# Key features interleaved by pairs of heads, a new start, shorter last sums and re-listed instructions in a four-block linear-attention and ReGLU kernel

## The chip, the cores and the metric

One core of one Trainium2 chip. The metric is device time of one execution in microseconds (us), median of several runs on chips whose runs of the kernel before agree within about 1%. All runs quoted here are of state fast. Engines: TensorE (PE in the profile), VectorE (DVE), ScalarE (ACT), GpSimd (POOL), SyncE (SP, which here issues DMA).

## The reference, cut to what matters

Four blocks on x of 2048 x 512, in bf16: attention, ReGLU, attention, ReGLU (called layers 0 to 3), each with a layer norm before and a residual after.

```
def _A_ref(x, wqkv, w_phi, wo):              # 32 heads of 16
    q, k, v = ...                            # x @ wqkv
    pq, pk = q @ w_phi, k @ w_phi            # per head
    phi_k = concat[softmax(pk), softmax(-pk)]   # over the 16 features of a head; phi_q alike
    kv = einsum("bhsf,bhsd->bhfd", phi_k, v);  z = einsum("bhsf->bhf", phi_k)
    o  = (phi_q @ kv) / (phi_q @ z + 1e-6)
    return o @ wo
def _B_ref(x, W_gate, W_up, W_down):         # F = 1376
    gate = relu(x @ W_gate);  return (gate * (x @ W_up)) @ W_down
```

All keys must be summed into kv before the first query can be answered: a barrier in each attention layer.

## The kernel before

The weights w_phi are folded into the key and query weights once (a block-diagonal BD per chunk of 128 columns). Instructions are recorded with cost figures (`ii` is the time until the engine takes the next, `lat` the time to the result) and put in order by a list scheduler when the program is built. The cost figures therefore change no instruction, but they do change the order on every engine.

The key stage, for each of 16 row tiles. Inside a chunk of 128 columns, feature f of head h sits at column 8f + h, so one head's 16 features are 8 columns (16 bytes) apart:

```python
for s in range(2):
    op("act", ... e.activation(ft.ap()[:, s, :], kt.ap(), ACT.Exp, scale=(1.0, -1.0)[s]), ...)
op("dve", ... e.tensor_reduce(zt.ap().rearrange("p (a h) -> p a h", h=8),
        ft.ap().rearrange("p s (c f h) -> p (s c) h f", f=16, h=8), AX.X, ALU.add), ..., ii=1105, lat=1185, name="Z")
op("dve", ... e.reciprocal(rt.ap(), zt.ap()), ...)
op("dve", ... e.tensor_tensor(ft..., ft..., rt.ap()...unsqueeze(2).to_broadcast([P, 8, 16, 8]), ALU.mult), ..., name="norm")
```

The barrier: sums on TensorE in four bursts of four tiles for each of three banks, then a masked copy of each of eight groups, and every R matmul (expq, the exponentials of the queries, times kvs, the masked sums) waits for all of them:

```python
for b, gs in enumerate(GROUPS):
    for q in range(4):                       # one op: 4 tiles x the bank's groups
        ...
    for j, (s, c) in enumerate(gs):          # 16 instructions in all
        op("dve", ... e.tensor_tensor(kvs[:, g, 0:128]..., pt..., mask2[:]..., ALU.mult), ...)
        op("dve", ... e.tensor_scalar(kvs[:, g, 128:136], mask2[:], pt..., 5e-7, ALU.mult, ALU.add), ...)
kvr[l] = [res(n, g) for g in range(8) for n in ("kvsn", "kvsd", "kvsm")]
```

The softmax here doesn't subtract the row's maximum and nothing guards it: scores larger than these inputs give would overflow.

## Time and profile before

442.8 us (440.2 to 444.4). The stage lengths below are read from the timeline view (start of the first, or end of the last, instruction of the kind named); the right-hand column tells which engine is full.

| stage, kernel before | from to, us | length | full engine |
|---|---|---|---|
| start, to the first key sum | 0 to 13.3 | 13.3 | none |
| layer 0's keys, to the last normalisation | 13.3 to 72.5 | 59.2 | VectorE |
| to the first gate matmul of layer 1 | 72.5 to 97.7 | 25.2 | none |
| layer 1, with the rest of layer 0, to the first key matmul of layer 2 | 97.7 to 226.9 | 129.2 | TensorE |
| layer 2's keys | 226.9 to 276.8 | 49.9 | VectorE |
| to the first gate matmul of layer 3 | 276.8 to 304.4 | 27.6 | none |
| layer 3 to the end | 304.4 to 438.1 | 133.7 | TensorE |

The windows view of the kernel before shows that. Each row is a stretch, its length, then busy us and instructions of the engines named in the first line, the share of full clock that TensorE was granted, the DMA share and GB/s:

```profile
core 0: us, PE busy (x) PEld busy (x) DVE busy (x) ACT busy (x) POOL busy (x), PEclk, DMA share, GB/s
13.26:72.47 59.21, 39.97 (x241) 21.06 (x244) 59.20 (x86) 27.68 (x58) 0.00 (x0) 0.86 0.50 130
72.47:97.69 25.22, 20.61 (x148) 11.22 (x150) 15.73 (x45) 20.03 (x64) 5.23 (x18) 1.00 0.16 32
97.69:226.92 129.23, 128.48 (x759) 70.71 (x773) 93.96 (x213) 48.21 (x165) 8.76 (x30) 1.00 0.23 43
226.92:276.79 49.87, 40.73 (x239) 22.15 (x243) 49.87 (x58) 29.77 (x62) 0.00 (x0) 0.93 0.07 14
276.79:304.35 27.56, 19.67 (x136) 10.65 (x137) 15.96 (x46) 16.22 (x56) 5.25 (x18) 0.94 0.14 29
304.35:438.10 133.75, 128.87 (x759) 70.87 (x772) 80.43 (x174) 42.50 (x138) 8.99 (x30) 1.00 0.21 46
```

VectorE is busy 59.20 of 59.21 us and 49.87 of 49.87 us in the two key stages; in the two long stages TensorE is. In the two transitions neither is full. What fills VectorE is in the groups view of the kernel before (busy us, mean ns of one, then idle time before and what ended it; `z<-phik` is the key sum, `phik<-phik,rz` the normalising multiply):

```profile
L583 DVE TENSOR_REDUCE z<-phik 128x64 f32<-128x1024 bf16 x32 | 61.2, 1948 | 2.0 <-ACT phik L582 2.0
L530 DVE BATCH_NORM_STATS2 stats<-x_sb 128x6 f32<-128x512 bf16 x64 | 42.8, 682 | 1.4 <-DMA x_sb<-in_A_x_dram 0.8
L586 DVE TENSOR_TENSOR phik<-phik,rz 128x1024 bf16<-128x1024 bf16 x32 | 20.0, 694 | 0.0
```

One key sum takes 1948 ns for 1024 elements, where bn_stats takes 682 ns for 512. The sum is the only one of the three that steps 16 bytes at each element.

The barrier, in the timeline of the kernel before (start, us, engine, line, instruction, number; in brackets the idle time before it and what ended it). The last normalisation starts at 71.76 us; the mask instructions end at 77.39 us:

```profile
71.76 0.70 DVE L586 TENSOR_TENSOR phik<-phik,rz 128x1024 bf16<-128x1024 bf16 x1
74.62 0.69 DVE L642 TENSOR_TENSOR kvs<-pb,mask 128x128 bf16<-128x128 f32 x3 [2.16 <-PE pb L631]
75.22 0.23 DVE L645 TENSOR_SCALAR kvs<-mask,pb 128x8 bf16<-128x8 bf16 x1
75.36 1.07 DVE L642 TENSOR_TENSOR kvs<-pb,mask 128x128 bf16<-128x128 f32 x5
76.35 1.04 DVE L645 TENSOR_SCALAR kvs<-mask,pb 128x8 bf16<-128x8 bf16 x7
```

### The profile page before, as it was taken

How to read it: one execution, taken by the hardware profiler on the slowest of the kernel's cores; microseconds unless marked ns; L12 is line 12 of the kernel's file. 1: busy time of each engine (PE TensorE's matmuls, PEld its weight loads, DVE VectorE, ACT ScalarE, POOL GpSimd, SP SyncE). 2: the span in 40 equal slices, each digit the busy share in tenths (PEclk: the TensorE clock that was granted, in tenths of full speed). 3: DMA queues.
4: the chain of work that ended last, by engine and by line, in shares of the span. 5: the costliest groups of instructions: out<-in, count | busy, mean ns of one | idle time of the engine just before them, and what ended most of it. 6: DMA issues, size and time to landing. Idle time of an engine off the chain costs nothing.

```text
span 438.1 us, 6374 instructions
## 1 busy us (share of the span) xinstructions
PE 384.3 (88%) x2308; PEld 210.2 (48%) x2348; DVE 322.6 (74%) x647; ACT 190.6 (44%) x556; POOL 31.6 (7%) x128
## 2 busy tenths in 40 slices
PE   3779718969999999999999966966999999999996
PEld 2323416437765545444443443624766544545442
DVE  6899998488989874636599999558897977334333
ACT  4748502966454431413149733546645443113200
POOL 3000000221110200000000000021111120000000
PEclk9969977999999999999999998889999999999999
DMA  6735930122321240112013000012342231201112
GB/s 179 170 61 87 326 107 0 25 49 49 77 57 38 60 62 12 37 24 38 13 36 62 0 1 0 1 24 49 49 86 49 48 62 37 48 13 36 25 36 72
DMA packets 69934, 24.18 MB, mean 55 GB/s; under 512 B 61360, under 2 KB 69904, under 8 KB 69904
## 3 DMA queue, kind: packets, MB, share of 16 engines
q1 hardware_dynamic: 68960, 23.38, 24.3%
q10 hardware_dynamic: 944, 0.41, 0.4%
q8 instruction: 18, 0.29, 0.3%
q14 instruction: 12, 0.10, 0.1%
HBM read 7.39 MB, written 2.10 MB: 22 GB/s over the span
## 4 chain that ended last, share of the span: by engine, by line
PE 61%; DVE 24%; DMA 5%; ACT 5%; issue 4%; POOL 0%; SPq 0%
PE pb L745 28%; PE pb L797 16%; DVE z L583 9%; PE pb L715 5%; DVE phik L586 3%; ACT phik L582 3%; DVE t L700 3%; PE pb L631 2%; DMA oT<-o 2%; DVE stats L530 2%; PE pb L666 2%; PE pb L773 2%; PE pb L577 2%; DMA yT<-y 2%; PE pb L611 2%
## 5 line engine op out<-in xcount | busy, mean ns | idle before, releaser
L752 ACT ACTIVATE gate<-pb 128x512 bf16<-128x512 f32 (+1 forms) x100 | 51.1, 511 | 89.2 <-PE pb L745 85.7
L745 PE MATMUL pb<-yT,Wg 128*128 128x512 bf16 (+1 forms) x391 | 81.1, 336 | 3.5 <-DMA yT<-y 3.0
L745 PE MATMUL pb<-yT,Wu 128*128 128x512 bf16 (+1 forms) x395 | 82.7, 336 | 0.2
L753 DVE TENSOR_TENSOR hT<-gate,pb 128x512 bf16<-128x512 bf16 (+1 forms) x100 | 56.0, 576 | 35.2 <-PE pb L745 34.7
L797 PE MATMUL pb<-Wd,hT 128*128 128x512 bf16 x314 | 75.3, 379 | 1.0 <-DMA hT<-hr 0.6
L583 DVE TENSOR_REDUCE z<-phik 128x64 f32<-128x1024 bf16 x32 | 61.2, 1948 | 2.0 <-ACT phik L582 2.0
L745 PEld LDWEIGHTS pb<-yT,Wg 128*128 128x128 bf16 x400 | 37.7, 98 | 34.8 <-DMA yT<-y 4.0
L745 PEld LDWEIGHTS pb<-yT,Wu 128*128 128x128 bf16 x400 | 38.2, 98 | 28.0 <-DVE t L700 0.2
L615 ACT ACTIVATE expq<-pb 128x512 bf16<-128x512 f32 x64 | 34.1, 614 | 38.2 <-PE pb L611 38.2
L797 PEld LDWEIGHTS pb<-Wd,hT 128*128 128x128 bf16 x320 | 31.0, 98 | 36.4 <-DMA hT<-hr 0.8
L530 DVE BATCH_NORM_STATS2 stats<-x_sb 128x6 f32<-128x512 bf16 x64 | 42.8, 682 | 1.4 <-DMA x_sb<-in_A_x_dram 0.8
L803 DVE TENSOR_TENSOR x_sb<-x_sb,pb 128x512 bf16<-128x512 bf16 x32 | 21.9, 684 | 26.3 <-PE pb L799 26.3
L577 PE MATMUL pb<-Wkp,yT 128*128 128x512 bf16 x126 | 33.7, 419 | 8.5 <-DMA yT<-y 7.5
L700 DVE TENSOR_TENSOR t<-pb,sm 128x384 bf16<-128x384 f32 x64 | 32.7, 548 | 8.4 <-POOL sm L691 8.4
L715 PE MATMUL pb<-wo,oT 128*128 128x512 bf16 x119 | 31.2, 388 | 8.6 <-DMA oT<-o 8.2
L582 ACT ACTIVATE phik<-pb 128x512 bf16<-128x512 f32 x64 | 33.9, 652 | 9.5 <-PE pb L577 9.1
L631 PE MATMUL pb<-vaug,phik 128*128 128x129 bf16 x256 | 20.3, 249 | 20.0 <-DVE phik L586 20.0
L718 DVE TENSOR_TENSOR x_sb<-x_sb,pb 128x512 bf16<-128x512 bf16 x32 | 21.9, 684 | 14.8 <-PE pb L715 14.8
L687 POOL TENSOR_TENSOR sm<-sm 128x64 f32<-128x64 f32 x32 | 10.4, 328 | 309.6 <-ACT sm L680 309.5
L611 PE MATMUL pb<-yT,Wqp 128*128 128x512 bf16 x123 | 30.3, 388 | 1.1 <-ACT expq L615 0.5
L533 ACT ACTIVATE lnv<-mv,eps 128x1 f32<-128x1 f32 (+2 forms) x56 | 16.2, 300 | 32.7 <-DVE mv L531 32.6
L631 PEld LDWEIGHTS pb<-vaug,phik 128*128 128x128 bf16 x256 | 18.9, 113 | 22.5 <-DVE phik L586 21.3
(56 smaller groups left out, 376.2 us busy)
## 6 DMA issues: line engine op xcount, KB each, us to landing
out_dram<-x_sb SPq DMA_DIRECT2D x16, 128.0 KB, 1.7
x_sb<-in_A_x_dram SPq DMA_DIRECT2D x3, 512.0 KB, 5.4
Wg<-in_B_W_gate_dram SPq DMA_DIRECT2D x2, 640.0 KB, 7.4
Wu<-in_B_W_up_dram SPq DMA_DIRECT2D x2, 640.0 KB, 8.4
Wd<-in_B_W_down_dram SPq DMA_DIRECT2D x1, 1280.0 KB, 12.2
yT<-y SPq DMA_TRANSPOSE x61, 2.5
wv<-in_A_wqkv_dram SPq DMA_DIRECT2D x1, 512.0 KB, 4.5
wo<-in_A_wo_dram SPq DMA_DIRECT2D x1, 512.0 KB, 4.3
```

The costliest lines, as they stand in the source:

```text
L530: op("dve", lambda e, t=t: e.bn_stats(stats[:, t, :], x_sb[:, t, :]), reads=[res("x", t)], writes=[res("st", t)], ii=600, lat=690, name=f" ...
L577: i = e.matmul(kt.ap(), src.ap()[:, ic, c0:c0 + 128], Wkp[:, ic, :], start=(ic == 0), stop=(ic == 3))
L582: op("act", lambda e, s=s: e.activation(ft.ap()[:, s, :], kt.ap(), ACT.Exp, scale=(1.0, -1.0)[s]), reads=[kr], writes=[fr2[s]], ii=477, la ...
L583: op("dve", lambda e: e.tensor_reduce(zt.ap().rearrange("p (a h) -> p a h", h=8), ft.ap().rearrange("p s (c f h) -> p (s c) h f", f=16, h= ...
L611: i = e.matmul(qt.ap(), Wqp[:, ic, c * 128:(c + 1) * 128], src.ap()[:, ic, :], start=(ic == 0), stop=(ic == 3))
L631: i = e.matmul(pt.ap()[:, j * 144:j * 144 + 129], ph[l, t][0].ap()[:, s, c * 128:(c + 1) * 128], va[l, t][0].ap()[:, c, 0:129], start=(t = ...
L700: return e.tensor_tensor(tt_.ap()[:, b, 0:384].rearrange("p (c h d) -> p c h d", h=8, d=16), pt.ap()[:, 0:432].rearrange("p (c w) -> p c w ...
L715: i = e.matmul(wt.ap(), oT_.ap()[:, c, :], wo[:, c, :], start=(c == 0), stop=(c == 3))
L745: i = e.matmul(pt.ap()[:, 0:n], W[:, ic, fc * 128:(fc + 1) * 128], src.ap()[:, ic, a * 128:b * 128], start=(ic == 0), stop=(ic == 3))
L752: op("act", lambda e: e.activation(st_.ap()[:, 0:n], gt.ap()[:, 0:n], ACT.Relu), reads=[gr], writes=[sr], ii=110 + n * .72, lat=230 + n * ...
L753: op("dve", lambda e: e.tensor_tensor(ht.ap()[:, a * 128:b * 128], st_.ap()[:, 0:n], ut.ap()[:, 0:n], ALU.mult), reads=[sr, ur], writes=[h ...
L797: i = e.matmul(pt.ap(), hT[l, s, fc].ap()[:, c:c + 128], Wd[:, fc, :], start=(fc == 0), stop=False)
```

## The change

Its intent: take VectorE time out of the key stages, and idle time out of the start and the transitions. It has five parts.

1. **Layout.** Heads interleaved by pairs: column 32a + 2f + b, so a head's features are 4 bytes apart.
2. **Start.** Key weights loaded plainly and transposed on TensorE; identity and masks made on VectorE; five matmuls on zeros on TensorE ahead of its first work (called the warm-up below).
3. **Sums.** The last tiles of the key-value sums in short bursts; mask instructions per bank (six for sixteen); R of a bank waits for its own bank.
4. **Transposes.** The first o and y tiles after each barrier are transposed on TensorE in place of DMA.
5. **Cost figures.** The scheduler's figures set anew, so everything is re-listed. (The key sum's figure stays at ii=1105; it took 1948 ns before the change.)

The diff, cut (`...`):

```diff
-    TR_ISSUE, TR_FIXED, TR_TIME = 900.0, 1500.0, 600.0
+    TR_ISSUE, TR_FIXED, TR_TIME = 1250.0, 1050.0, 250.0
...
-    o_id = op("pool", lambda e: e.affine_select(ident[:], ones[:], [[1, 128]], ALU.is_equal, 0.0, ...), ...)
+    op("dve", lambda e: e.memset(rowi[:, 0:1], 0.0), ..., name="row0")
+    for k in range(5): ...                       # rowi = 0..31 by doubling; transposed to a column
+    for q in range(4):
+        op("dve", ... e.tensor_scalar(ident[sl, sl], rowi[sl, :], colf[sl, :], None, ALU.is_equal), ...)
...
-    load_wT(t_wk, c_wkT, 512, 0)                 # DMA transposes of the key weights
+    load_wk(0)                                   # plain loads
+    for k in range(5): op("pe", ... e.matmul(pt_w.ap(), wm.ap()[:, 0:128], wm.ap(), ...), name="warm")
+    ...                                          # per 128 rows: 4 TensorE transposes, 1 copy
...
-        ... ft.ap().rearrange("p s (c f h) -> p (s c) h f", f=16, h=8), AX.X, ALU.add)
+        ... ft.ap().rearrange("p s (a f b) -> p (s a) b f", f=16, b=2), AX.X, ALU.add)
-        rt.ap().rearrange("p (a h) -> p a h", h=8).unsqueeze(2).to_broadcast([P, 8, 16, 8]), ALU.mult), ii=650, lat=740
+        rt.ap().rearrange("p (a b) -> p a b", b=2).unsqueeze(2).to_broadcast([P, 32, 16, 2]), ALU.mult), ii=602, lat=695
...
+    BURSTS = [(0, 4), (4, 8), (8, 12), (12, 14), (14, 15), (15, 16)]
-            reads=[eq...] + kvr[l]
+            reads=[eq...] + kvr[l][b]
-            op("act", cp, ..., ii=170, lat=290, name="sm")
+            op("act", cp, ..., ii=92, lat=212, name="sm")
...
+PE_Y = {(0, 0), (0, 1), (0, 2), (1, 0), (1, 1), (2, 15), (3, 0), (3, 1)}
+PE_O = {(0, 0), (0, 1), (2, 0), (2, 1)}
```

## The prediction

> **What bounds it now.** By the windows view VectorE (DVE) is busy 53.7 of 54 us in 13-67 us (layer 0's key features) and 33.0 of 33 us in 240-273 us (layer 2's). Between, TensorE (PE) is: 55.6 of 56 us in 104-160 us and 66.6 of 67 us in 160-227 us. PE is busy 384 of 438 us and idles mainly in 0-13 (7 us), 13-67 (19), 81-104 (4), 240-273 (9) and 286-312 (7). The gain can only come from those holes.
>
> The groups view's second entry is the key softmax sum (TENSOR_REDUCE z): 32 times 1.95 us, 61 us. Two back to back take 3.79 us, so 1.88 us per 1024 elements, while bn_stats takes 0.60 us per 512. The sum walks a stride of 8 bf16 = 16 bytes.[...]
>
> **What the change does.**
> 1. Head pairs: the sum walks 4 bytes[...]. Estimate from bn_stats: 1.1 us issue (1.2 us as one record), saving 0.78 us x 32 = 25 us of VectorE. All 32 lie in the two VectorE-bound stages. The normalising multiply (0.69 us[...]) keeps adjacent bf16 pairs, so I expect it unchanged. Layer 0: -12.5 us, wholly critical. Layer 2: the same, but PE has about 35 us of key, value and sum matmuls in a stage that shrinks from 48 to 36 us, and query matmuls (about 20 of 64) now done in its holes come later: about -10 net.
> 2. Start: the four transposing loads of the key weights issue over 1.27-6.48 us; the first key matmul starts at 10.2 us, first sum at 13.3. Plain loads, PE transposes and copies should give about 7 and 9 us[...]. VectorE gets two more copies. Net -2 to -3 us. The identity on VectorE is worth nothing: affine_select took 0.29 us.
> 3. Short last sums and masks per bank: after the last normalisation (72.4 us) the first R matmul waits until 77.4: 32 matmuls (2 us), then 16 mask instructions (2.8 us). Now 8 matmuls and 6 instructions, R of bank 0 waiting only for its own: about -2.5 us each layer. PE fills part of that wait with query matmuls, so about -1.5 counts.
> 4. PE transposes for the first o and y tiles: DMA transposes of 2.4-2.5 us at 82.8 and 95.2 (and 288.1, 301.8) stand in the chain of waits; PE (0.25) plus ACT copy (0.6) plus hand-overs is about 1.2. About -2 us per layer, bounded by PE's holes of 4 and 7 us.
> The GLU stages (104-227, 312-438) are PE-bound and unchanged.
>
> **Sum.** -12.5 -2.5 -10 -3 -4 = -32, from 442.8: **410 us**. Eight in ten: 400 to 420. Faster by over 2%: 0.97; within 2%: 0.025; slower: 0.005.
>
> **What would show it.** z near 1.2 us; phik normalisation still near 0.69; first key matmul near 7 us; VectorE-bound stages ending near 57 us after the start (was 72) and about 35 us long in layer 2 (was 48); 3+3 mask instructions per layer; PE busy down a little[...], span down by PE's lost idle; GLU stages same length.
>
> **What would make it wrong.**[...] The program is list-scheduled from changed costs, so all orders shift: query matmuls moving into the key stage would give 5-8 us more; a worse order could lose as much. VectorE idling for x loads or for the y transposes in layer 0, now that it runs ahead. Layer 2 becoming PE-bound earlier than I count.

The -2.5 us of the start hold a term of -1 us for the warm-up matmuls. The 1.1 us for the sum (from bn_stats, 0.60 us per 512) and the 1.2 us for a tile transposed on TensorE are estimates.

## The result, and the profile after

407.6 us (406.9 to 408.4), against 442.8 us for the kernel before in the same rounds: ratio 0.921, 95% interval 0.916 to 0.926. A ratio is always the mean time of one kernel's fast runs over that of the other's of the same rounds, so it is not quite the ratio of the medians quoted. A second set of runs of the changed kernel on another chip gave 408.1 us and 0.923 (0.919 to 0.926).

The same stretches of the changed kernel in the windows view:

```profile
14.38:60.47 46.09, 38.46 (x235) 20.83 (x234) 44.63 (x80) 26.90 (x57) 0.00 (x0) 0.85 0.58 150
60.47:83.21 22.74, 21.30 (x166) 12.18 (x165) 13.78 (x35) 20.37 (x65) 4.61 (x16) 1.00 0.06 12
83.21:213.82 130.61, 130.29 (x773) 70.72 (x772) 93.54 (x213) 49.07 (x168) 10.38 (x33) 1.00 0.21 39
213.82:251.72 37.90, 37.83 (x259) 20.56 (x258) 37.68 (x58) 29.57 (x61) 0.00 (x0) 1.00 0.12 26
251.72:271.94 20.22, 18.78 (x145) 10.61 (x143) 13.77 (x36) 17.07 (x59) 4.62 (x16) 1.00 0.07 14
271.94:406.20 134.26, 130.26 (x773) 70.84 (x771) 80.80 (x174) 42.89 (x140) 10.15 (x33) 1.00 0.20 46
```

Layer 0's keys take 46.1 us (was 59.2), layer 2's 37.9 (was 49.9). There TensorE is now as full as VectorE: 37.83 and 37.68 of 37.90 us. The query matmuls alone, by the windows view of the kernel before and then of the changed one, mostly stayed in layer 2's key stage: 20 before and 16 now, counted by their weight loads, since the trace of before holds 17 matmuls to 20 weight loads (PE and PEld busy, clock, DMA share, GB/s):

```profile
226.92:276.79 49.87, 4.66 (x17) 2.25 (x20) 0.93 0.07 14
```

```profile
213.82:251.72 37.90, 3.78 (x16) 1.49 (x16) 1.00 0.12 26
```

The transition after layer 2's keys fell from 27.6 to 20.2 us and TensorE idles only 1.4 us of it (was 7.9). The long TensorE stages are 1.4 and 0.5 us longer. The start did not get shorter: the first key sum begins at 14.4 us (was 13.3).

The groups view of the changed kernel, same columns as before:

```profile
L611 DVE TENSOR_REDUCE z<-phik 128x64 f32<-128x1024 bf16 x32 | 37.2, 1189 | 0.2 <-ACT phik L610 0.2
L614 DVE TENSOR_TENSOR phik<-phik,rz 128x1024 bf16<-128x1024 bf16 x32 | 19.8, 677 | 0.0
```

The sum fell from 1948 to 1189 ns, 24.0 us over 32 of them; the multiply did not move. The barrier in the timeline of the changed kernel, where the last normalisation ends at 60.47 us:

```profile
59.24 1.23 DVE L614 TENSOR_TENSOR phik<-phik,rz 128x1024 bf16<-128x1024 bf16 x2
63.61 1.02 DVE L667 TENSOR_TENSOR kvs<-pb,mask 128x384 bf16<-128x384 f32 x2 [3.15 <-PE pb L659]
64.55 0.26 DVE L670 SCALAR_TENSOR_TENSOR kvs<-pb,mask 128x24 bf16<-128x24 f32 x2
64.73 0.41 DVE L667 TENSOR_TENSOR kvs<-pb,mask 128x256 bf16<-128x256 f32 x1
65.06 0.16 DVE L670 SCALAR_TENSOR_TENSOR kvs<-pb,mask 128x16 bf16<-128x16 f32 x1
```

The masks are cheaper (1.6 us in place of 2.8), but VectorE waits 3.15 us for the last sums, in place of 2.16. On TensorE query matmuls stood in front of the last sums before, too (2.74 us at a granted clock of 0.93); now they take 3.88 us (at 0.71), and four more split the sums.

What the whole barrier costs shows in the first R matmuls, of layer 0 and of layer 2, in the timeline of the kernel before:

```profile
77.45 1.17 PE L666 MATMUL pb<-kvs,expq 128*128 128x144 bf16 x16
282.57 1.17 PE L666 MATMUL pb<-kvs,expq 128*128 128x144 bf16 x16
```

And in the timeline of the changed kernel:

```profile
64.90 1.16 PE L692 MATMUL pb<-kvs,expq 128*128 128x144 bf16 x16
253.63 1.16 PE L692 MATMUL pb<-kvs,expq 128*128 128x144 bf16 x16
```

From the end of the last normalisation that is 4.4 us in layer 0 (was 5.0) and 1.9 us in layer 2 (was 5.8).

### The profile page after: what moved, and what is told of

Its sections match the earlier page's. It is cut to its first block, busy times and chain, and to the rows that moved or that the text cites. A ratio compares the mean times of both kernels' runs of the same rounds, so it can differ in the third digit from the quotient of the medians.

```text
span 406.2 us, 6510 instructions
## 1 busy us (share of the span) xinstructions
PE 386.3 (95%) x2405; PEld 210.6 (52%) x2405; DVE 297.2 (73%) x635; ACT 194.1 (48%) x567; POOL 31.8 (8%) x119
## 4 chain that ended last, share of the span: by engine, by line
PE 66%; DVE 17%; ACT 9%; DMA 3%; issue 2%; POOL 1%
PE pb L782 30%; PE pb L834 17%; ACT expq L643 5%; DVE z L611 4%; PE pb L752 4%; PE pb L605 3%; DVE stats L558 3%; PE pb L659 3%; PE pb L623 2%; DVE phik L614 2%; PE pb L810 2%; DMA oT<-o 2%; PE pb L639 2%; PE pb L836 2%; PE pb L692 2%
## 5 line engine op out<-in xcount | busy, mean ns | idle before, releaser
L782 PE MATMUL pb<-yT,Wg 128*128 128x512 bf16 (+1 forms) x400 | 83.6, 337 | 0.0
L790 DVE TENSOR_TENSOR hT<-gate,pb 128x512 bf16<-128x512 bf16 (+1 forms) x100 | 56.1, 573 | 35.6 <-PE pb L782 35.2
L834 PEld LDWEIGHTS pb<-Wd,hT 128*128 128x128 bf16 x320 | 31.2, 98 | 37.9
L840 DVE TENSOR_TENSOR x_sb<-x_sb,pb 128x512 bf16<-128x512 bf16 x32 | 21.8, 681 | 37.3 <-PE pb L836 37.3
L643 ACT ACTIVATE expq<-pb 128x512 bf16<-128x512 f32 x64 | 35.0, 606 | 17.1 <-PE pb L639 17.1
L610 ACT ACTIVATE phik<-pb 128x512 bf16<-128x512 f32 x64 | 35.1, 672 | 6.1 <-PE pb L605 6.0
L611 DVE TENSOR_REDUCE z<-phik 128x64 f32<-128x1024 bf16 x32 | 37.2, 1189 | 0.2 <-ACT phik L610 0.2
L605 PE MATMUL pb<-Wkp,yT 128*128 128x512 bf16 x128 | 31.8, 398 | 4.3 <-DMA yT<-y 4.3
L639 PE MATMUL pb<-yT,Wqp 128*128 128x512 bf16 x128 | 31.9, 390 | 1.0 <-DVE t L726 0.8
L752 PE MATMUL pb<-wo,oT 128*128 128x512 bf16 x128 | 32.2, 379 | 0.5 <-DMA oT<-o 0.5
L623 PE MATMUL pb<-wv,yT 128*128 128x512 bf16 x128 | 31.1, 387 | 0.0
L572 DVE TENSOR_SCALAR y<-x_sb,mv,rstd 128x512 bf16<-128x512 bf16 x64 | 25.4, 407 | 4.5 <-ACT rstd L563 2.9
```

The costliest lines, as they stand in the source:

```text
L605: i = e.matmul(kt.ap(), src.ap()[:, ic, c0:c0 + 128], Wkp[:, ic, :], start=(ic == 0), stop=(ic == 3))
L610: op("act", lambda e, s=s: e.activation(ft.ap()[:, s, :], kt.ap(), ACT.Exp, scale=(1.0, -1.0)[s]), reads=[kr], writes=[fr2[s]], ii=477, la ...
L611: op("dve", lambda e: e.tensor_reduce(zt.ap().rearrange("p (a b) -> p a b", b=2), ft.ap().rearrange("p s (a f b) -> p (s a) b f", f=16, b= ...
L623: i = e.matmul(vt.ap(), src.ap()[:, ic, c0:c0 + 128], wv[:, ic, :], start=(ic == 0), stop=(ic == 3))
L639: i = e.matmul(qt.ap(), Wqp[:, ic, c * 128:(c + 1) * 128], src.ap()[:, ic, :], start=(ic == 0), stop=(ic == 3))
L643: op("act", lambda e, g=g: e.activation(es[g][0].ap(), qt.ap(), ACT.Exp, scale=(1.0, -1.0)[g]), reads=[qr], writes=[es[g][1]], ii=477, lat ...
```

## The experiments

Twelve kernels, all correct, beside runs of the kernel before. The stage lengths that the text below uses, read from the timeline of one profile each:

| stage, us | before | changed | pairs only | pairs, new costs | relieved |
|---|---|---|---|---|---|
| start, to the first key sum | 13.3 | 14.4 | 14.0 | 12.6 | 14.3 |
| layer 0's keys | 59.2 | 46.1 | 49.4 | 49.5 | 44.0 |
| to the first gate matmul | 25.2 | 22.7 | 26.7 | 24.5 | 20.0 |
| layer 1 | 129.2 | 130.6 | 132.0 | 129.7 | 130.7 |
| layer 2's keys | 49.9 | 37.9 | 37.8 | 38.4 | 37.9 |
| to the first gate matmul | 27.6 | 20.2 | 27.9 | 23.2 | 20.2 |
| layer 3 | 133.7 | 134.3 | 133.7 | 134.0 | 134.0 |

**Theory:** the 35 us are mainly the sum's steps of 16 bytes, in stages bounded by VectorE; the rest is idle time of TensorE around the barriers. **Rivals:** the new order brings most of it; or a longer step simply costs more, whatever the 16 bytes.

### Head pairs alone

```diff
 kernel before
-  ft "p s (c f h) -> p (s c) h f", f=16, h=8      (sum, multiply, BD and mask alike)
+  ft "p s (a f b) -> p (s a) b f", f=16, b=2
```

> The kernel before with nothing but the head-pair layout (sum, normalising multiply, block-diagonal weights, mask); the order of instructions on every engine is that of before. Theory (the sum's 16-byte stride is what cost): z falls from 1.95 to 1.19 us, 32 x 0.76 = 24 us of VectorE, nearly all critical: 419 us (415 to 423). Rival (the new order and the transition stages bring most of the 35 us): at most 12 us off, 430 us or more.

421.7 us, ratio 0.954 (0.950 to 0.958): 20.4 us faster. The order of TensorE, ScalarE, GpSimd and DMA is row by row that of before; on VectorE three rows differ, at the start. The groups view of this variant:

```profile
L584 DVE TENSOR_REDUCE z<-phik 128x64 f32<-128x1024 bf16 x32 | 37.2, 1190 | 2.5 <-ACT phik L583 2.5
```

So more than half of the gain is this alone and the first rival falls. Of the 24 us taken from VectorE, 3.6 did not arrive. Layer 2's keys give 12.1. Layer 0's give only 9.8, since VectorE, which had no idle time there, now idles 1.9 of 49.4 us: by the view of waits 0.5 us for an exponential and 1.4 us for DMA transposes that hold the buffers of the normalised x. Then the first transition and layer 1 grow by 1.5 and 2.8 us; TensorE's granted clock over layer 1 was 0.99 in this profile (1.00 before). The stages of this profile add up to 16.6 us less than before, not 20.4, because it is of one of the slowest runs of the variant, and the profile of before is of one of the fastest of that kernel.

### The changed kernel without pairs

```diff
 changed kernel
-  ..."p s (a f b) -> p (s a) b f", f=16, b=2
+  ..."p s (a f b) -> p (s a) b f", f=16, b=8      (BD in one instruction again)
```

> The changed kernel with eight heads interleaved again, as before; order the same but for a few rows at the start. Theory: z back at 1.95 us, +24 us: 431 us (427 to 435). Rival (order and transitions): less than +15 us, 422 or less. If this and the pairs-only run add up with the same size, the layout is independent of the rest.

431.7 us, 0.976 (0.973 to 0.979): 0.053 to 0.055 of before, 24 us, slower than the changed kernel. The groups view of this variant:

```profile
L611 DVE TENSOR_REDUCE z<-phik 128x64 f32<-128x1024 bf16 x32 | 61.4, 1948 | 1.0 <-ACT phik L610 1.0
```

With the rest of the change in place the layout is worth all of its 24 us.

### Four heads

```diff
 changed kernel
-  f=16, b=2
+  f=16, b=4
```

> The changed kernel with four heads interleaved: the sum steps 8 bytes[...].[...] z stays at 1.19 us and the time at 408 us (0.923 of before). Rival (cost grows with the step): z between 1.3 and 1.7 us and 411 to 424 us.

408.1 us, 0.926 (0.923 to 0.930). The groups view of the variant with four heads:

```profile
L611 DVE TENSOR_REDUCE z<-phik 128x64 f32<-128x1024 bf16 x32 | 37.3, 1192 | 0.2 <-ACT phik L610 0.2
L614 DVE TENSOR_TENSOR phik<-phik,rz 128x1024 bf16<-128x1024 bf16 x32 | 19.8, 681 | 0.0
```

A step of 8 bytes costs the same as one of 4: 1192 and 1189 ns. The second rival falls: the cost does not grow with every longer step. Where between 8 bytes and 16 (1948 ns) it sets in was not tried, and these runs do not show what causes it.

### One head

```diff
 changed kernel
-  f=16, b=2
+  f=16, b=1
```

> The changed kernel with heads not interleaved: the sum walks adjacent elements, but the multiply's second factor is one value repeated 16 times. Theory: z stays at 1.19 us, the multiply falls from 0.68 to about 1.2 us[...], 32 x 0.53 = 17 us of VectorE: 422 us (417 to 425). Rival (the multiply does not care): 408 us.

424.8 us, 0.963 (0.961 to 0.966). The groups view of the variant with one head:

```profile
L611 DVE TENSOR_REDUCE z<-phik 128x64 f32<-128x1024 bf16 x32 | 37.3, 1192 | 1.6 <-ACT phik L610 1.5
L614 DVE TENSOR_TENSOR phik<-phik,rz 128x1024 bf16<-128x1024 bf16 x32 | 36.9, 1212 | 0.0
```

The sum is no faster at 2 bytes than at 4 or 8, and the multiply takes nearly twice as long: 1212 in place of 677 ns, 17.1 us over 32, and 17 us in the time. Of the layouts tried, two adjacent heads are thus the smallest that serves both instructions: the sum took 1189 to 1192 ns with 2, 4 and 8 bytes between features and 1948 ns with 16, the multiply 677, 681 and 694 ns with two, four and eight heads side by side and 1212 ns with one.

### DMA transposes again

```diff
 changed kernel
-PE_Y = {(0, 0), (0, 1), (0, 2), (1, 0), (1, 1), (2, 15), (3, 0), (3, 1)};  PE_O = {(0, 0), (0, 1), (2, 0), (2, 1)}
+PE_Y = {(0, 0), (0, 1), (0, 2)};  PE_O = set()
```

> The changed kernel with the first o and y tiles of each later block transposed by DMA again. As predicted: +2 us per layer, 411.5 us (409.5 to 414). Rival: the stage from the last normalisation of layer 2 to the first gate matmul fell by 7.3 us where 3.5 was predicted; if these transposes are the reason, +7 to +10 us: 415 to 418, with a gap for DMA of 2 us or more twice in each such stage.

410.2 us, 0.928 (0.925 to 0.932): 0.006 to 0.007 of before, about 2.6 us, slower than the changed kernel, with intervals that touch. The last transition takes 21.8 in place of 20.2 us, not 27. So the TensorE transposes alone are not what took 7.3 us off it.

### Old sums

```diff
 changed kernel
-    BURSTS = [(0, 4), (4, 8), (8, 12), (12, 14), (14, 15), (15, 16)];  reads ... kvr[l][b];  masks per bank
+    four bursts of four tiles;  reads ... kvr[l];  masks per group
```

> The changed kernel with the key-value sums in four bursts of four tiles, 16 mask instructions, and every R matmul waiting for all masks, as before. As predicted: +1.5 us per layer, 410.6 us (409 to 413). Rival: if the 7.3 us of layer 2's transition come from here, +5 to +8 us: 413 to 416.

411.6 us, 0.931 (0.929 to 0.934): 4 us slower. The last transition takes 21.3 us. Not this part alone either. In this and the run before, the scheduler lists everything anew after the edit (by the traces, some 130 and 140 of 340 groups of like matmuls on TensorE stand elsewhere), so part of what it takes away is filled with other work.

### Old cost figures, and new ones on top of the pairs alone

```diff
 changed kernel                            | head pairs alone
-TR_ISSUE ... = 1250.0, 1050.0, 250.0; ... | -TR_ISSUE ... = 900.0, 1500.0, 600.0; ...
+TR_ISSUE ... = 900.0, 1500.0, 600.0; ...  | +TR_ISSUE ... = 1250.0, 1050.0, 250.0; ...
```

> The changed kernel's operations, listed with the old cost figures, so only the order of instructions differs (238 rows of TensorE). Theory: with layout 24, sums 4.0 and transposes 2.6 us of the 34.5 accounted for, the order is worth the missing 2 to 5 us: 410 to 413 us, most of it between the last normalisation and the first gate matmul. Rival (the order is worth nothing): within 1 us of the control.

411.0 us, 0.929 (0.926 to 0.932), against 0.923 (0.919 to 0.926) of the control: about 2.9 us, with intervals that just touch. The last transition takes 22.4 in place of 20.2 us.

> The kernel before with head pairs and the new cost figures: nothing else of the change. Against the pairs-only run (421.7 us, 0.954 of before) only the order differs. Theory: 2 to 5 us less, 417 to 420 us (0.943 to 0.949 of before). Rival (no worth of its own): 0.951 to 0.957.

413.6 us, 0.936 (0.932 to 0.940), against 0.954 of the pairs alone: 7.8 us from nothing but another order of the same instructions, more than expected. Where it went shows in the last transition, in the windows view of the pairs alone:

```profile
259.84:287.75 27.91, 20.28 (x135) 10.81 (x135) 16.09 (x46) 16.16 (x56) 5.22 (x18) 0.88 0.14 29
```

And the pairs with the new cost figures, from the windows view of that variant:

```profile
254.66:277.83 23.17, 17.07 (x134) 9.60 (x133) 15.51 (x45) 15.28 (x55) 5.26 (x18) 1.00 0.17 35
```

The same 135 or so matmuls, 4.7 us shorter: TensorE idles 6.1 in place of 7.6 us, and is busy 17.07 in place of 20.28 us at a granted clock of 1.00 in place of 0.88. The table above shows 2.2 and 2.3 us more in the first transition and in layer 1. What set the clock, and how much of the 3.21 us of busy time it made, is not shown: there is one profile of each.

So the order, the sums and the transposes look like three remedies for the same idle time in front of the first gate matmul. On top of the pairs alone, the order takes 7.8 us; taken back from the changed kernel, it costs 2.9, the sums 4.0 and the transposes 2.6. The sums and the transposes were not tried on top of the pairs alone, so this is argued.

### The control, the old start, no warm-up

```diff
 control: the changed kernel itself
 old start: - load_wk(ic), TensorE transposes and copies   + load_wT(t_wk, c_wkT, 512, ic), loads in the old order
 no warm-up: - for k in range(5): op("pe", ... name="warm")
```

> The changed kernel itself, as a control on the same chip as the next three: 407.6 us (406.5 to 409.5). Its first key matmul, at 11.7 us in the first profile and 13.2 us in two variants with the same instructions at the start, should move by 1 to 2 us between profiles[...].

> The changed kernel with the key weights transposed on their way in by DMA and the loads in the old order; identity on VectorE and warm-up stay. Theory after seeing the profile: the plain loads land at 4.3 to 7.5 us and two more copy steps follow, so the TensorE way gains nothing: within 1.5 us of the control, first key matmul at 10 to 12 us. Rival (the prediction: the new start is worth 2 to 3 us, hidden by something else): 2 us or more slower than the control.

> The changed kernel without the five warm-up matmuls, the order otherwise the same. As predicted they were worth 1 us: 409 us (0.925). Rival: within 0.5 us (0.922 to 0.924), since VectorE, not TensorE, sets the pace from the first sum on[...].

Control: 408.1 us, 0.923. Old start: 409.5 us, 0.926 (0.922 to 0.930). No warm-up: 409.0 us, 0.928 (0.925 to 0.931), to be held against the variant with four heads, 408.1 us and 0.926. None of these is clear of noise: by their intervals the new start can be worth some 4 us at most, the warm-up some 3.

Why not more: in the first profile of the changed kernel the plain loads of the key weights took 2.7 to 4.7 us to land, the last at 6.8 us, only 1.2 us before the last transposing load of the kernel before (8.0). TensorE idled 1.1 us for them and 0.6 us for the identity before its transposes. Then come two rounds of copies in place of one, the last copy behind other work of VectorE, so the key weights are ready at 11.2 us (10.2 before). Last, the new order puts four value matmuls in front of the first key matmul (0.86 us there, 1.71 us in the control). The first key matmul started at 10.2 us in the kernel before, 11.7 and 12.8 us in two profiles of the changed one, 10.1 us with the old start; in all nine profiles with plain loads and the new cost figures at 11.5 to 14.0 us, in the four with transposing loads at 9.6 to 10.9. So the new start was rather a loss at that point. That the old start is no faster as a whole may be chance: in its profile one DMA transpose in the last transition took 4.5 us in place of 2.4, and this transition 22.1 in place of 20.2. With the warm-up in place the pace of the first key matmuls varies, too. These matmuls in the timeline of the control, which has the warm-up:

```profile
12.81 1.91 PE L605 MATMUL pb<-Wkp,yT 128*128 128x512 bf16 x4
```

And in the timeline of the variant without it:

```profile
11.82 1.03 PE L598 MATMUL pb<-Wkp,yT 128*128 128x512 bf16 x4
```

Four matmuls took 1.91 us with, and 1.03 us without the warm-up. In the first profile of the changed kernel, and in those of the variants with four heads and with VectorE relieved, all with the warm-up (five matmuls in 2.31 us), they took 1.03 us; in the kernel before, which has none, eight took 3.51 us. So in these profiles the pace does not follow the warm-up. Nor does the granted clock tell the control from the first profile: the windows view has 1.00 for the first key matmuls of both. What sets the pace is not shown.

### Relieved VectorE

```diff
 changed kernel
-    identity from rowi, coli, colf on VectorE
+    op("pool", ... e.memset(ones[:], 1.0)); op("pool", ... e.affine_select(ident[:], ones[:], ...), ii=300, lat=400)
-    r_wq = compose(t_wq, c_wqT, Wqp, "Wqp", ["dve", "act", "dve", "act"])
+    r_wq = compose(t_wq, c_wqT, Wqp, "Wqp", ["act"] * 4)
```

> Meant to beat both: the changed kernel with the identity made on GpSimd (0.3 us there, some 2.5 us less on VectorE) and both VectorE copies of the query weights (1.28 us inside layer 0's key stage) moved to ScalarE. If VectorE bounds that stage throughout: 1.5 to 3 us faster, 405 to 406.5 us (0.917 to 0.920 of before). If the identity fell in time that VectorE waited anyway and the order shifts, within 1 us of 408.

404.1 us (402.9 to 405.3), 0.917 (0.914 to 0.921): better than expected, and faster than all eight runs of the changed kernel (406.9 to 408.7) and the four of the variant with four heads on the same chip (407.6 to 410.2). It beats the kernel before, and by 1% the variant with four heads on the same chip (0.926, intervals apart), whose time is that of the changed kernel; against the changed kernel's own ratios from other chips (0.921 and 0.923) the intervals still touch. What changed shows in the query matmuls alone, by the windows view (PE and PEld busy, clock, DMA share, GB/s); these rows are layer 0's keys and the transition of the control:

```profile
15.88:61.85 45.97, 2.85 (x10) 1.30 (x11) 0.93 0.52 139
61.85:84.27 22.42, 12.31 (x52) 4.30 (x49) 1.00 0.06 12
```

And the same two stages of this variant, again the query matmuls alone:

```profile
14.29:58.30 44.01, 9.84 (x44) 4.17 (x44) 1.00 0.60 156
58.30:78.34 20.04, 4.09 (x16) 1.70 (x16) 0.83 0.06 13
```

In the changed kernel the two copies of query weights on VectorE are listed behind most of the key work, at 54.0 us, so no query matmul can start before 55.3 us, and the first does at 57.6. With the copies on ScalarE the first starts at 19.3 us: 44 query matmuls run in the key stage, where TensorE has idle time, in place of 10, and 16 in the transition in place of 52. The move of the identity shows no effect at the start: VectorE then waits 3.0 us for TensorE's transposes, and the first key matmul starts at 11.6 us (11.7 in the changed kernel). The two edits were not run one by one, and the scheduler listed TensorE's work anew, so neither the split of the 1% between them nor the query matmuls as its cause is shown.

## Why the prediction was right or wrong

The time was right (410 predicted, 407.6 measured, range 400 to 420), and its main term too. Several other terms of the sum were not; that their errors cancelled is luck.

- **The key sums, "32 x 0.78 = 25 us of VectorE" and 1.2 us each: right.** 1189 ns, 24.0 us in all; 20.4 us alone and 24 us with the rest in place. That the multiply keeps its pace with pairs was right as well (677 ns); at one head, tried later, it does not (1212 ns).
- **Layer 2's keys, "about -10 net": too cautious.** They gave 12.0 us. The prediction counted TensorE's limit in this stage, and TensorE is indeed full there now (37.83 of 37.90 us). The step that failed is "query matmuls (about 20 of 64) now done in its holes come later", for which it took away 2 us: by their weight loads 16 of 20 still run in this stage. The other matmuls take about 34 of the 37.9 us, at a granted clock of 1.00 (0.93 before), and leave room for them.
- **The start, "-2 to -3 us, first key matmul near 7 us": wrong.** The first key matmul came at 11.7 us, later than before (10.2), and undoing the loads changed the time by no more than noise (0.926 and 0.923). The step that failed was the path behind the loads: the last plain load landed at 6.8 us, by itself little before the 7 us predicted for the first key matmul; transposes, two rounds of copies and a wait for VectorE made the key weights ready at 11.2 us only, and four value matmuls then came first. The -1 us for the warm-up failed, too: the first four key matmuls took 1.03 or 1.91 us with it and 1.03 us without it, and the time without it (0.928) is within noise of that with it (0.926). The place of the identity showed no effect at the start, as predicted (it was not moved alone).
- **Short sums and masks per bank, "-1.5 us" per layer, and the transposes, "-2 us" per layer: the mechanism right, the sizes shifted.** Undone one at a time, the sums cost 4.0 us and the transposes 2.6, where 3 and 4 stood. By layer the size was off more: "about -2.5 us each layer" for the wait before the first R matmul was 0.5 us in layer 0, where query matmuls fill the wait, and 3.9 us in layer 2; the profiles before and after differ in order as well.
- **The order, named only as something that might go wrong by 5 to 8 us: a term of its own.** It is worth 7.8 us on top of the pairs alone, 2.9 us with the rest in place. It has the largest part in the last transition, which fell by 7.3 us where 3.5 was predicted: 4.7 us by the order alone (27.9 to 23.2 us, on top of the pairs). Taken back from the changed kernel, the order costs 2.2 us there, the transposes 1.6 and the sums 1.1.
- **By layers.** Up to layer 2's first key matmul -18.5 us was predicted and -13.1 measured (226.9 to 213.8 us); from there -13.5 predicted and -18.8 measured. In the first part layer 0's keys gave what was predicted (-13.1 for -12.5), but the start (+1.1 for -2.5), the transition (-2.5 for -3.5) and layer 1 (+1.4 for 0) did not. The right total hides two errors of 5 us. (These are two profiles, 31.9 us apart where the medians are 35.2, since that of before is of a fast run.)

What stays open: where between 8 and 16 bytes the sum gets slow, and why. How the 35 us split between the parts is not unique, since they seem to fill the same idle time. The start and the warm-up are not resolved below about 4 and 3 us. What set TensorE's lower granted clock in the last transition of before (0.94, after 1.00) was not tested, nor the kernel before re-listed with the sum's true cost.

## What to carry to other kernels

Lay out data for both instructions that walk it. Here a VectorE sum of 1024 bf16 took 1189 to 1192 ns with its elements 2, 4 or 8 bytes apart and 1948 ns at 16 (1.6 times as much; nothing between was tried), and the multiply with a broadcast factor 677 to 694 ns with two, four or eight adjacent 16-bit values and 1212 ns with one. In a list-scheduled kernel, new cost figures and the re-listing that follows are a change in themselves: test them alone, before counting what an edit brought. When one engine bounds a stage, look for small instructions on it that hold back another engine's work: with two copies of 0.68 us (and the identity) moved off VectorE, 34 more query matmuls ran inside the key stage, and the time was 1% below that of the variant with four heads.
